# Where GpSimd splits the first half's maxima, and in what order SyncE loads their rows

## The chip, the cores and the metric

The kernel runs on one core of a Trainium2 chip. The core has five engines with an instruction queue each: TensorE (PE in the profile; its weight loads are a row of their own, PEld), VectorE (DVE), ScalarE (ACT), GpSimd (POOL) and SyncE (SP), which in this kernel issues every transfer (DMA). Engines wait for one another through semaphores. The metric is the time of one execution in microseconds (us); lower is better. Times of single instructions are taken from one profiled execution, counted from the start of its span.

## The reference

The program computes a gated mix of attention and a gated linear unit, for one sequence of 2048 tokens of width 512, in 32-bit floats:

```python
x = A_x                                            # 1 x 2048 x 512
g = sigmoid((x * gate_w).sum(-1, keepdims=True))
# a: attention with 32 heads of width 16, a full softmax over 2048 keys
q, k, v = split_heads(x @ wqkv)
p = softmax(einsum("bhqd,bhkd->bhqk", q, k) * 16 ** -0.5)
a = merge_heads(einsum("bhqk,bhkd->bhqd", p, v)) @ wo
# b: gated linear unit, hidden width 1792
b = (sigmoid(x @ w_gate) * (x @ w_up)) @ w_down
return g * a + (1 - g) * b
```

## The kernel before

**Precision.** TensorE works on a reduced 32-bit form. A number is therefore split into a high part h (a cast) and a low part l (the number less h), and a product is made of three matmuls: h by h, h by l, l by h. The splits of weights run on GpSimd, a cast and a subtraction for each buffer (`split_later`, lines 136 and 133).

**Attention.** Heads are taken in 16 pairs. The rows of Q and K of a pair lie in the tiles QS and KS: the first head of the pair in partitions 0 to 63, the second in 64 to 127, so that matmuls of 64 rows for the two heads can run in TensorE's two halves at the same time. For a softmax over 2048 keys the largest score of each query is needed first. `sm_step` computes scores with the queries on the partitions (line 281) and VectorE takes their maxima (line 283) into `stat`. When all 64 maxima of half a pair (8 tiles of 128 queries, 2 heads, 4 blocks of 512 keys) are there, VectorE reduces them once more (line 287) and transposes them (line 289) into a small tile `mt`, which is noted in `mrow`. `put_max` takes it from there: GpSimd splits it into high and low part (line 308 the cast, line 299 the subtraction), SyncE stores the result to memory (`max_d`, line 301) and loads it again, turned into rows, behind the head's rows in QS: four loads (line 305), high and low part for the second head, then for the first. With these rows in place the scores of `st_part` (line 645) come out of TensorE with the maximum already taken off, and ScalarE takes the exponential (line 647).

**The value stage.** Before the main loop comes a stage that computes the values v for all 16 tiles of 128 tokens, two tiles at a time (t = 0, 2, ... 14). It stands at about 35 to 87 us. Each tile is a `Sum` of 12 products, cut into two halves of the contraction, LOW (partitions 0 to 63) and UP. While one tile does its LOW half on one half of TensorE, the other does its UP half on the other; after 12 steps (m = 0 to 11) they change places. Because two halves of TensorE must not write one bank out of turn, `turn` puts an empty GpSimd instruction between, the token (line 170): it waits for the last matmul of the first 12 steps, and the next step's matmuls (line 159) wait for it. Into these steps other work is woven:

- `first_max` issues the first 40 pairs of maxima, at even distances from step 20 of 192 on. The last of the first half of pair 0, (0, 0), falls at t = 12, LOW, m = 9. Right after that step `put_max((0, 0))` is called, which puts its GpSimd instructions in GpSimd's queue ahead of the token of t = 12.
- `work(1.3)` after each 12 steps from t = 12 on takes GpSimd work of an estimated 1.3 us from a list: here the splits of the weights qk1 (two buffers, a cast and a subtraction each).
- `next(ahead)` at t = 14 issues the first four scores of pair 0, for the second head, after the steps LOW 10, UP 1, UP 4 and UP 7. They need the rows of the maxima.

**The main loop** follows, 256 steps of which 246 have the same pattern (`STEADY`): in each, maxima of a later pair, scores and exponentials of the present one, the values' sums (line 778) and six steps for each half of a dense product (`fill`, a list of further products: first more of Q and K, then the hidden layer of the linear unit). The dense products take their weights two buffers at a time (`raw_weights`, line 107 the load, into two buffers that are reused). The loads of the weights qk2 are asked for when the first dense product begins, right ahead of the loop. After the loop comes a tail with the linear unit's second product and the output.

**Queues.** The order of the instructions of TensorE, ScalarE, VectorE and GpSimd is the order of the program. SyncE's is not: a planner orders the transfers by estimated times, within what their dependencies allow. Each queue is in order: an instruction that waits holds all behind it.

Of the kernel before, what the change touches and what calls it, by code (L numbers as in the profile page):

```python
# [22 lines left out]
SYNC = mybir.DependencyInfo(mybir.DependencyClass.Sync, mybir.DependencyReason.DATA)  # L23

S, D, H, DH, F = 2048, 512, 32, 16, 1792
P = 128
KT = D // P
NS = S // P
# [14 lines left out]
LOW, UP = 0, 1  # L43
# [3 lines left out]
def gated_mix(ctx, tc, x, xT, wqk, wv, wo, w_gate, w_up, w_down, gate_w, out):  # L47
    nc = tc.nc
    pe, act, dve, pool, sp = nc.tensor, nc.scalar, nc.vector, nc.gpsimd, nc.sync
# [42 lines left out]
    def big(name, dt=F32):  # L92
        return keep.tile([P, 2048], dt, name=name, tag="big", bufs=4)
# [8 lines left out]
            hi.tensor_copy(h, src)  # L102
        return lo.tensor_tensor(l, src, h.bitcast(F32), ALU.subtract)  # L103

    def raw_weights(src, shape, name):
        raw = keep.tile(shape, F32, name=name + "r", tag="wr", bufs=2)
        sp.dma_start(raw, src)
        return raw, shape, name

    def raw_qk(n, b):  # L110
        return raw_weights(wqk[n, b], [P, 2, 2, P], f"qk{n}_{b}")

    def q_and_k(ws):
        return [[(h[:, i, k, :], l[:, i, k, :]) for h, l in ws for k in range(2)] for i in range(2)]
# [1 line left out]
    def raw_cols(src, n, name):  # L116
        return raw_weights(src[n], [P, KT, P], name)
# [50 lines left out]
    def turn(*runs):  # L168

        token = pool.nop()  # L170
        tc.add_manual_dep(token.ins, runs[-1].last.ins.name, SYNC, reason=SHARED)
        for r in runs:
            r.token = token
# [3 lines left out]
    def work(length):  # L177
        while length > 0.3 and (later or slow):
            cost, step = (later or slow).pop(0)
            step()  # L180
            length -= cost
# [7 lines left out]
    QS, KS = zip(*[(big(f"qs{b}", F32R), big(f"ks{b}", F32R)) for b in range(2)])  # L189
# [57 lines left out]
    raw, xr, w_qk = [], {}, []  # L247
    for b in range(2):
        raw.append(raw_qk(0, b))
        xr[0] = load_x(0, xr.get(0), range(2 * b, 2 * b + 2))  # L250
# [9 lines left out]

    stat = {}
    mrow = {}
    for m in mpads:
        pool.memset(m, 0.0)

# [26 lines left out]
    def put_max(half):  # L292

        p, i = half
        mt = mrow.pop(half)
        hl = keep.tile([P, 2, 32], F32R, name=f"mhl{p}_{i}", tag="mhl", bufs=2)

        def low():
            pool.tensor_tensor(hl[:, 1, :], mt, hl[:, 0, :].bitcast(F32), ALU.subtract)
            d = max_d[2 * p + i]  # L300
            sp.dma_start(d.rearrange("k r a j -> (k r) a j"), hl.bitcast(F32))
            for b in (1, 0):
                for a in range(2):
                    r = 64 * b + 3 * DH + a
                    sp.dma_start(QS[p % 2][r:r + 1, i * 1024:(i + 1) * 1024].rearrange(
                        "o (t k j) -> o t k j", t=8, k=4).bitcast(F32),
                        d[:, 8 * b:8 * b + 8, a, :].rearrange("k t j -> t k j").unsqueeze(0))
        return [(0.2, lambda: pool.tensor_copy(hl[:, 0, :], mt)), (0.25, low)]  # L308
# [63 lines left out]
    def filling():  # L372
# [5 lines left out]
        def raws(kind, n):  # L378
            if kind == "qk":
                return [raw_qk(n, b) for b in range(2)]  # L380
            if kind == "far":
                both = []
                for m in range(2):
                    raw = keep.tile([P, KT, P], F32, name=f"far{m}{n}r", tag="wr", bufs=2)
                    sp.dma_start(raw[:, 2:], gu_w[m][n][:, 2:])
                    both.append(raw)
                return both
            if kind == "down":
                return [raw_weights(w_down[f * P:(f + 1) * P, :], [P, D], f"wd{f}") for f in range(2)]
            if kind == "heads":  # L390
                return [raw_weights(wo[k * P:(k + 1) * P, :], [P, D], f"wo{k}") for k in range(2)]
            m, i = n
            return [raw_cols(gu_w[m], i + a, f"{kind}{m}_{i + a}") for a in (0, HF)]
# [185 lines left out]
    def first_max():  # L579
        if first:  # L580
            j, i = first.pop(0)
            one = sm_step(j)
            one(0, i)
            one(1, i)
# [36 lines left out]
    def tokens(t):  # L621
        return [((xh[:, k, t * P:(t + 1) * P], xl[:, k, t * P:(t + 1) * P]), w_v[k]) for k in range(KT)]

    def put_v(t, o, engine):
        to = v[:, t, :].rearrange("p (h c) -> p h c", c=VW)[:, :, :DH]
        o = o.rearrange("p (h c) -> p h c", c=DH)
        if engine is act:
            act.activation(to, o, AF.Copy)  # L628
        else:
            engine.tensor_copy(to, o)  # L630
# [21 lines left out]
    for t in range(0, NS, 2):  # L652
        two = [Sum(bankv(), tokens(t + a)) for a in range(2)]
        for g in (LOW, UP):
            for m in range(3 * KT):
                if 12 * (t + g) + m >= 20 + (192 - 20) * (2 * LEAD - len(first)) // (2 * LEAD):
                    first_max()
                two[0].half(g)
                two[1].half(1 - g)
                if (0, 0) in mrow:  # L660
                    for _, step in put_max((0, 0)):
                        step()
                if t == NS - 2 and (g, m) in ((LOW, 10), (UP, 1), (UP, 4), (UP, 7)):
                    next(ahead)
            if g == LOW:
                turn(*two)
            if t >= 12:
                work(1.3)
        if t < NS - 2:
            for a in range(2):  # L670
                put_v(t + a, two[a].o, act)
# [165 lines left out]
    for k in range(NPER):  # L837
        n = 2 * k
# [3 lines left out]
        if 78 <= k < 126:  # L842
            t, r = divmod(k - 78, 6)
# [174 lines left out]
```

## Time and profile before

| | |
|---|---|
| time, median of 3 runs | 1697.17 us (1696.29 to 1697.56) |
| the profiled execution's own time | 1697.63 us |
| its span, first to last instruction | 1695.8 us |
| PE busy | 1686.1 us (99%) |
| DVE busy | 1447.3 us (85%) |
| ACT busy | 1357.0 us (80%) |
| POOL busy | 881.5 us (52%) |

The span is 1.8 us shorter than the time of the execution that it belongs to; what lies around it is the start and the end of the program. A row of a timeline gives start, duration, engine, line and operation, the tile written and the tiles read, shapes, a count (x2 is two instructions merged), and in brackets how long the engine had been idle and what ended that. In a table of waits stands who waited for whom, then the total in us, the number of times and the longest. Two rows with the same start are the two halves of TensorE. SPq and POOLq are instructions of those engines' sequencers, such as the issue of a transfer or an empty instruction.

### The profile page before, as it was taken

What the parts mean: (1) busy time and instruction counts of PE and PEld (TensorE: products, weight loads), DVE (VectorE), ACT (ScalarE), POOL (GpSimd) and SP (SyncE); (2) the same over time, 40 slices, a digit from 0 to 9 for tenths busy, and PEclk for the clock granted to TensorE, in tenths of its full rate; (3) what the DMA queues carried; (4) which work ended last, traced back from release to release, by engine and by line L of the source; (5) the groups of instructions that cost most, each with busy time, mean ns of one, the idle gap of its engine ahead of it and who ended that gap; (6) DMA issues with size and microseconds to landing.
All of it is one profiled execution on the core that took longest, in us unless ns stands there. A gap on an engine that the chain in (4) does not pass through costs nothing.

```text
span 1695.8 us, 34520 instructions
## 1 busy us (share of the span) xinstructions
PE 1686.1 (99%) x12509; PEld 1031.9 (61%) x12509; DVE 1447.3 (85%) x2333; ACT 1357.0 (80%) x2643; POOL 881.5 (52%) x862
## 2 busy tenths in 40 slices
PE   9999999999999999999999999999999999999999
PEld 7755555555555556555555555555555555567887
DVE  6888888888889989999888888889988888897643
ACT  4188888888988889888888989889898888974321
POOL 1034343447665555554666667676666767653110
PEclk9999999999999999999999999999999999999999
DMA  7411424253756352543635353535353434378752
GB/s 235 109 40 58 95 64 95 64 126 138 202 170 143 114 119 90 114 114 107 192 100 138 107 144 104 142 108 134 108 126 107 126 120 144 129 239 269 269 195 72
DMA packets 126922, 223.51 MB, mean 132 GB/s; under 512 B 23520, under 2 KB 33504, under 8 KB 123872
## 3 DMA queue, kind: packets, MB, share of 16 engines
q1 hardware_dynamic: 126752, 221.31, 45.1%
q8 instruction: 98, 1.61, 0.4%
q14 instruction: 72, 0.59, 0.1%
HBM read 131.33 MB, written 89.92 MB: 130 GB/s over the span
## 4 chain that ended last, share of the span: by engine, by line
PE 96%; DVE 2%; DMA 1%; issue 0%; ACT 0%; POOL 0%; SPq 0%; POOLq 0%; DVEq 0%; ACTq 0%
PE dn L159 30%; PE sm L778 27%; PE sm L281 12%; PE st L645 7%; PE sm L645 5%; PE sm L963 4%; PE st L281 3%; PE st L159 2%; PE dn L963 2%; PE st L609 1%; PE st L146 1%; PE st L963 1%; DMA gul<-gu_d 1%; PE sm L146 1%; DVE gul L713 0%
## 5 line engine op out<-in xcount | busy, mean ns | idle before, releaser
L283 DVE TENSOR_REDUCE stat<-sm 128x1 f32<-128x512 f32 x1310 | 849.4, 684 | 153.0 <-PE sm L645 127.3
L647 ACT ACTIVATE p<-st 128x512 f32<-128x512 f32 x1020 | 617.8, 652 | 1.9 <-PE st L159 0.9
L647 ACT ACTIVATE p<-sm 128x512 f32<-128x512 f32 x1026 | 608.7, 630 | 0.2 <-PE sm L645 0.2
L281 PE MATMUL sm<-ks,qs 48*128 48x512 f32 x1310 | 515.9, 435 | 0.0
L283 DVE TENSOR_REDUCE stat<-st 128x1 f32<-128x512 f32 x738 | 482.6, 682 | 0.1
L778 PE MATMUL sm<-p,v 128*17 128x512 f32 x4032 | 482.1, 595 | 0.0
L645 PE MATMUL st<-qs,ks 64*128 64x512 f32 x1020 | 427.1, 419 | 0.2 <-DVE stat L283 0.2
L645 PE MATMUL sm<-qs,ks 64*128 64x512 f32 x1026 | 427.0, 419 | 0.1
L281 PEld LDWEIGHTS sm<-ks,qs 48*128 48x128 f32 x1310 | 233.9, 184 | 289.6 <-DVE stat L283 207.7
L795 POOL TENSOR_TENSOR sum<-sum,part 128x512 f32<-128x512 f32 x224 | 288.9, 1290 | 182.1 <-PE sm L645 162.9
L281 PE MATMUL st<-ks,qs 48*128 48x512 f32 x738 | 291.5, 395 | 0.0
L783 ACT ACTIVATE part<-sm 128x512 f32<-128x512 f32 x215 | 128.7, 599 | 132.7 <-issue 106.6
L778 PEld LDWEIGHTS sm<-p,v 128*17 128x17 f32 x4032 | 93.6, 96 | 227.0 <-issue 156.6
L645 PEld LDWEIGHTS st<-qs,ks 64*128 64x128 f32 x1020 | 187.7, 184 | 30.5 <-issue 3.4
L645 PEld LDWEIGHTS sm<-qs,ks 64*128 64x128 f32 x1026 | 189.1, 185 | 9.3 <-issue 4.3
L511 POOL TENSOR_TENSOR chain<-chain,chain 128x512 f32<-128x512 f32 x84 | 108.4, 1290 | 114.7 <-PE sm L645 105.0
L281 PEld LDWEIGHTS st<-ks,qs 48*128 48x128 f32 x738 | 137.7, 187 | 1.3 <-ACT v L628 0.3
L511 POOL TENSOR_TENSOR had<-chain,had 128x512 f32<-128x512 f32 x84 | 108.2, 1288 | 57.2 <-PE sm L645 41.9
L511 POOL TENSOR_TENSOR side<-side,side 128x512 f32<-128x512 f32 x28 | 36.2, 1292 | 92.6 <-PE sm L645 82.6
L573 ACT ACTIVATE chain<-dn 128x512 f32<-128x512 f32 x112 | 77.8, 694 | 0.0
L103 POOL TENSOR_TENSOR ol<-ot,oh 128x1024 fp32r<-128x1024 f32 (+1 forms) x8 | 16.4, 2054 | 100.9 <-ACT oh L100 87.3
L308 POOL CAST mhl<-mt 128x32 fp32r<-128x32 f32 x32 | 7.4, 232 | 104.0 <-DVE mt L289 104.0
(837 smaller groups left out, 3208.4 us busy)
## 6 DMA issues: line engine op xcount, KB each, us to landing
gul<-gu_d SPq DMA_DIRECT2D x56, 512.0 KB
had<-gu_d SPq DMA_DIRECT2D x84, 256.0 KB
gu_d<-had SPq DMA_DIRECT2D x84, 256.0 KB
gu_d<-side SPq DMA_DIRECT2D x56, 256.0 KB
qs<-q_d SPq DMA_DIRECT2D x90, 128.0 KB
ks<-k_d SPq DMA_DIRECT2D x90, 128.0 KB
pv_d<-sum SPq DMA_DIRECT2D x32, 256.0 KB
gu_d<-far SPq DMA_DIRECT2D x28, 256.0 KB
```

The costliest lines, as they stand in the source:

```text
L146: pe.matmul(o, a, b, start=(i == 0), stop=(i == len(ops) - 1))
L159: mm = pe.matmul(self.o, a[rows], b[rows], start=(self.n == 0), stop=(self.n == 2 * len(self.ops) - 1))
L281: pe.matmul(t, qs[r:r + KM, qt * P:(qt + 1) * P], ks[r:r + KM, g * 512:(g + 1) * 512], start=True, stop=True)
L283: dve.tensor_reduce(stat[half][:, b, qt % 8, g:g + 1], t, axis=AX.X, op=ALU.max)
L511: pool.tensor_tensor(to, u, w, ALU.add)
L573: leave = lambda e, o: act.activation(e, o, AF.Copy)
L645: pe.matmul(o, ks[r:r + KR, (kt + a) * P:(kt + a + 1) * P], qs[r:r + KR, q0:q0 + 512], start=True, stop=True)
L647: act.activation(pt[:, 2 * a + c, :], o, AF.Exp, scale=DH ** -0.5)
L778: pe.matmul(o[32 * c:32 * c + VW, :], v[:, 2 * k % 16 + a, h * VW:(h + 1) * VW], pts[c // 2][:, 2 * a + c % 2, :], start=(a == 0), stop=(a ...
L783: act.activation(e, o, AF.Copy)
L795: pool.tensor_tensor(s, s, e, ALU.add)
L963: pe.matmul(down[t], a, b, start=(f == 0 and m == 0), stop=(f == NF - 2 and m == 5))
```

## The change

It has four parts:

1. `put_max((0, 0))` is called at t = 12 after the step UP, m = 2, in place of right after LOW, m = 9. GpSimd's split of the first half's maxima so stands behind the token of t = 12 in its queue.
2. GpSimd's work from the list is taken in two portions of 2.6 at the step UP, m = 6 of t = 12 and t = 14, in place of four portions of 1.3 after each 12 steps.
3. The two loads of the weights qk2 get a dependency on the last of the four loads of the maxima's rows of (0, 0), so that they wait until it has landed.
4. The first four scores are issued after the steps LOW 11, UP 2, UP 5 and UP 8, each one step later.

```diff
-    def raw_weights(src, shape, name):
+    def raw_weights(src, shape, name, behind=None):
         raw = keep.tile(shape, F32, name=name + "r", tag="wr", bufs=2)
-        sp.dma_start(raw, src)
+        load = sp.dma_start(raw, src)
+        if behind is not None:
+            tc.add_manual_dep(load.ins, behind.ins.name, SYNC, reason="weights behind the rows of the maxima")
         return raw, shape, name

     def raw_qk(n, b):
-        return raw_weights(wqk[n, b], [P, 2, 2, P], f"qk{n}_{b}")
+        return raw_weights(wqk[n, b], [P, 2, 2, P], f"qk{n}_{b}", rows_in[0, 0] if n == 2 else None)
...
+    rows_in = {}
...
-                    sp.dma_start(QS[p % 2][r:r + 1, i * 1024:(i + 1) * 1024].rearrange(
+                    rows_in[p, i] = sp.dma_start(QS[p % 2][r:r + 1, i * 1024:(i + 1) * 1024].rearrange(
...
                 two[0].half(g)
                 two[1].half(1 - g)
-                if (0, 0) in mrow:
+                if (0, 0) in mrow and g == UP and m == 2:
                     for _, step in put_max((0, 0)):
                         step()
-                if t == NS - 2 and (g, m) in ((LOW, 10), (UP, 1), (UP, 4), (UP, 7)):
+                if t == NS - 2 and (g, m) in ((LOW, 11), (UP, 2), (UP, 5), (UP, 8)):
                     next(ahead)
+                if t >= 12 and m == 6 and g == UP:
+                    work(2.6)
             if g == LOW:
                 turn(*two)
-            if t >= 12:
-                work(1.3)
```

## The prediction

> **What bounds the kernel now.** I read the page first for its busy shares, then the table of waits for TensorE (PE) alone, then PE's busy time by stretches, then the timelines of the few microseconds in which the waits stand, and last the chain of waits there. The page:
>
> ```profile
> span 1695.8 us, 34520 instructions
> PE 1686.1 (99%) x12509; PEld 1031.9 (61%) x12509; DVE 1447.3 (85%) x2333; ACT 1357.0 (80%) x2643; POOL 881.5 (52%) x862
> ```
>
> PE is busy for 1686.1 of 1695.8 us. This change removes no matmul, so all it can take away is idle time of PE, of which there are 1695.8 - 1686.1 = 9.7 us in the whole program. The table of waits says what ended the idle times (who waited, for whom: us in total, times, longest):
>
> ```profile
> PE dn L159 <- POOLq L170: 1.6, 1, 1.6
> ...
> PE dn L645 <- DMA qs<-max_d: 0.9, 1, 0.9
> ```
>
> These are the two places that the change touches: a half sum of the value stage (L159) that waits for GpSimd's token (L170), and the first score (L645) that waits for the loads of the maxima's rows (DMA qs<-max_d). Together that is 2.5 us, 0.15% of the time. The windows' busy times show where nothing is left to take (stretch, its length, busy time of PE with its count, then the other engines):
>
> ```profile
> 87.27:1460.00 1372.73, 1372.51 (x10802) 795.01 (x10802) 1224.00 (x2066) 1220.16 (x2439) 808.68 (x810) 1.00 0.43 119
> ```
>
> From the first step of the main loop on, PE is busy 1372.51 of 1372.73 us. Whatever is gained or lost ahead of 87.27 us goes straight through this stretch to the end, because PE's own order sets it.
>
> Now PE's timeline at both places (start, duration, engine, line, operation):
>
> ```profile
> 65.46 0.40 PE L159 MATMUL st<-wv_h,xl 64*128 64x512 f32 x2
> 65.97 0.50 PE L159 MATMUL st<-wv_h,xh 64*128 64x512 f32 x2
> ...
> 72.34 0.39 PE L159 MATMUL st<-wv_l,xh 64*128 64x512 f32 x1
> 72.57 0.39 PE L159 MATMUL st<-wv_h,xl 64*128 64x512 f32 x1
> 74.58 0.50 PE L159 MATMUL dn<-wv_h,xh 64*128 64x512 f32 x1 [1.61 <-POOLq L170]
> 74.92 0.39 PE L281 MATMUL sm<-ks,qs 48*128 48x512 f32 x2
> ...
> 80.94 0.39 PE L159 MATMUL st<-wv_l,xh 64*128 64x512 f32 x2
> 82.22 0.47 PE L645 MATMUL dn<-qs,ks 64*128 64x512 f32 x1 [0.89 <-DMA qs<-max_d]
> 82.56 0.58 PE L159 MATMUL st<-wv_h,xl 64*128 64x512 f32 x2
> 83.25 0.51 PE L159 MATMUL st<-wv_h,xh 64*128 64x512 f32 x2
> ```
>
> Step m of a half is one such row; a row starts 0.23 us after the last (72.34 to 72.57). Between LOW's last step and UP's first stands the token. It cost 65.97 - 65.46 = 0.51 us at t=10, but 74.58 - 72.57 = 2.01 us at t=12. Why, the other engines say (DVE, POOL and SP in the order of time):
>
> ```profile
> 73.98 0.21 DVE L289 STREAM_TRANSPOSE mt<-mpad 128x32 f32<-128x32 f32 x1
> 74.26 0.21 POOL L308 CAST mhl<-mt 128x32 fp32r<-128x32 f32 x1 [55.39 <-DVE mt L289]
> 74.55 0.25 POOL L299 TENSOR_TENSOR mhl<-mt,mhl 128x32 fp32r<-128x32 f32 x1
> 74.83 0.34 SPq L301 DMA_DIRECT2D max_d<-mhl  x1
> 75.44 1.29 POOL L133 TENSOR_TENSOR qk_0l<-qk_0r,qk_0h 128x512 fp32r<-128x512 f32 x1
> 76.75 0.35 SPq L107 DMA_DIRECT2D qk_0r<-in_wqk_dram  x1
> 77.36 1.29 POOL L133 TENSOR_TENSOR qk_1l<-qk_1r,qk_1h 128x512 fp32r<-128x512 f32 x1
> 78.67 0.33 SPq L107 DMA_DIRECT2D qk_1r<-in_wqk_dram  x1
> 79.10 2.90 SPq L305 DMA_DIRECT2D qs<-max_d  x4
> ```
>
> GpSimd's cast L308 waits for VectorE's transposed maxima (mt, ready at 73.98 + 0.21 = 74.19), and the token behind it in POOL's order waits too. SyncE issues the store of the maxima at 74.83, then two weight loads, each only once GpSimd has read the buffer that it overwrites (76.73 and 78.65), and only then the four row loads. The chain of waits at this place (start, duration, what), which goes on with the score at 82.22:
>
> ```profile
> 77.36 1.30 POOL qk_1l L133
> 78.67 0.33 SPq L107
> 79.10 0.80 SPq L305
> 79.95 2.13 DMA qs<-max_d
> ```
>
> **The change, part by part.**
>
> The token (split moved behind UP's step m=2 at t=12). The token then waits only for LOW's last matmul, as at t=10: 0.51 instead of 2.01 us, a gain of 1.50. The cast itself stays at 74.26, since the transposed maxima set it and they depend on matmuls ahead of the token. VectorE's next maxima come 1.50 us sooner (matmul at 73.42 instead of 74.92), while it is at the final reduction until 74.19; it has a backlog then, and it does not shrink, because a maximum takes 0.62 us (next fence: ten in 6.23 us), two take 1.24, and two are asked for every 172 / 40 = 4.3 steps and their own, 5.3 x 0.23 = 1.22 us. But VectorE starts them at 74.3 at the earliest, 0.9 us after the matmul, and the four banks allow PE one such pair more, 1.22 us, ahead of it. So I count nothing; if PE had to wait for a bank, it would be tenths of a microsecond.
>
> ```profile
> 75.35 6.23 DVE L283 TENSOR_REDUCE stat<-sm 128x1 f32<-128x512 f32 x10 [1.16 <-PE sm L281]
> ...
> 122.27 0.33 SPq L301 DMA_DIRECT2D max_d<-mhl  x1
> ...
> 124.80 0.68 SPq L305 DMA_DIRECT2D qs<-max_d  x1
> ```
>
> The row loads. The store is issued at 74.83 as before. At the second such pair (fence above) the first row load follows 124.80 - 122.27 = 2.53 us after the store, which I take for the store's landing; so here it goes out at 74.83 + 2.53 = 77.36 instead of 79.10. The second row load follows 79.95 - 79.10 = 0.85 later, 78.21, and from it to the released score are 82.22 - 79.95 = 2.27 us. The rows of the first scores are there at 80.48 instead of 82.22.
>
> The first scores one step later. PE reaches LOW's m=10 at 80.94 - 1.50 = 79.44. Then come two maxima, m=11 and the score, 0.23 each: the score is ready at 79.44 + 0.69 = 80.13 and waits until 80.48, 0.35 us. After such a wait the next pair of matmuls came 82.56 - 82.22 = 0.34 later, so UP's first step starts at 80.82. The token costs nothing there: m=11 starts at 79.90, and 79.90 + 0.51 = 80.41 is earlier. Before, UP's first step started at 83.25. The three parts together gain 83.25 - 80.82 = 2.43 us. With rows that land at once the token would set it, 83.25 - 80.41 = 2.84. With rows that land no sooner than now, 82.22 + 0.34 = 82.56, the gain is 0.69.
>
> The Trainium skill, "DMA: Bandwidth & Descriptors", section "Latency and other measured facts", says that the fixed cost of a DMA is mostly the round trip to memory and becomes smaller with a lighter memory load. By that rule the row loads, with no weights in flight beside them, should land in less than the 2.27 us of the trace, and the sum would move from 2.43 towards 2.84; no run so far shows it, and I keep 2.43.
>
> What is behind the new wait. The first weight load waits for the last row load, and SyncE's queue behind it. That queue has nothing more to issue until 100.59; the other rows of this fence are the first readers of what comes later now, and ScalarE at the end of the value stage:
>
> ```profile
> 86.55 0.60 ACT L647 ACTIVATE p<-st 128x512 f32<-128x512 f32 x1 [0.56 <-PE st L645]
> 87.46 1.08 ACT L628 ACTIVATE v<-st 128x512 f32<-128x512 f32 x2 [0.32 <-PE st L159]
> 93.66 0.40 PE L159 MATMUL dn<-xh,qk_1h 64*128 64x512 f32 x1
> ...
> 100.59 0.38 SPq L233 DMA_DIRECT2D q_d<-qe  x1
> ...
> 124.12 0.60 POOL L136 CAST qk_0h<-qk_0r 128x512 fp32r<-128x512 f32 x1
> ```
>
> The last row load goes out two places behind the second, at 78.21 + 2 x 0.73 = 79.7 (four took 2.90 us), and lands by 82; GpSimd reads the weights at 124.12, so 40 us cover them. The work of 2.6 at m=6 takes the two splits (0.60 + 1.29 each) in three operations and one: the first three go behind the row split of t=12, from 74.80 to 77.3, ahead of t=14's token (79.90 + 0.39 = 80.3); the fourth, qk_1l, goes behind that token and ends near 81.6. TensorE first uses qk_1 at 93.66, 91.2 with the gain taken off. So both cost nothing, with 9 us of cover; without it, 1.29 us for the late operation. The last score comes 0.23 us later against the end of its stage, and its exponential on ScalarE, which ended at 86.55 + 0.60 = 87.15, then ends 0.08 us short of the copy of the last value tiles at 87.46. That costs nothing; an exponential that is 0.1 us later still would cost about as much.
>
> Sum: 1697.63 us was the profiled execution (span 1695.8), 0.46 over the median of 1697.17. A gain of 2.43 gives 1695.2 against the profiled execution's own time and 1694.7 against the median. The bounds above give 1694.3 (rows at once) and 1696.5 (rows no sooner).
>
> **Rivals.**
>
> The rows come no sooner. Then the score's wait swallows most of what the token gains. It would be so if the store's landing took 82.22 - 80.48 = 1.74 us longer than at 122.27, or if the planner of SyncE's queue kept something ahead of the rows. For it: the landing of the store at 74.83 itself is not shown. Against it: the manual dependency leaves no other transfer in the queue there. Gain 0.69, time 1696.5.
>
> Slower: SyncE's queue is not in program order. The loads of a head pair are planned by estimates, and a shifted estimate could move one behind a longer wait at one of the 14 later pair changes. Pair 2's loads and the longest wait of that queue:
>
> ```profile
> 181.88 4.64 SPq L242 DMA_DIRECT2D ks<-k_d  x6
> ...
> SPq L233 <- POOL qe L133: 152.4, 23, 18.5
> ```
>
> They are issued by 186.5; pair 2's maxima start 22 steps of 1372.73 / 246 = 5.58 us after 87.27, near 210, so some 21 us of lead are left after a landing like the 2.53 above. One wait of 18.5 is covered; it decides only where a load falls behind two, and one such stall of about 2 x 18.5 - 21 = 16 us would give 1697.2 - 2.4 + 16 = 1711. From 5.8 us on the kernel is slower by 0.2%.
>
> Faster than the sum: the main loop gets tighter, because ScalarE's backlog in its first step or VectorE's phase is another. Against it: PE idles for only 0.22 us of that stretch, so it would have to come from matmuls that overlap better. But 0.004 us on each of 246 steps is 1 us, and with that the time is 1693.7.
>
> **How the numbers follow.** What a measurement of this kernel can tell from no change is about 0.2%, 3.4 us, and the whole PE idle time that the change addresses is less. The sum as worked out, 0.63, with 1694.2 to 1695.6 as its own range; rows no sooner, 0.16; the planner's loss, 0.09; the tighter loop, 0.12, most of it below 1693.8. So faster by over 0.2% 0.12, within 0.78, slower 0.10. The range is 1693.6 to 1697.0: it takes in the bounds and half of the tighter loop.
>
> **What would show it.** The wait of PE for POOLq L170 goes from the table, and VectorE's idle of 1.16 us ahead of 75.35 with it. SyncE's order reads store, four row loads, two weight loads, with the first row load near 77.4. The score's wait for qs<-max_d is at most 0.35 us, and the main loop's first matmul stands near 84.8 instead of 87.27. The prediction is wrong if that point moves by 2.4 us and the end doesn't, if the rows leave SyncE later than 78, or if PE waits for DVE stat in the value stage.

## The result and the profile after

The changed kernel takes 1694.22 us (median of 22 runs, 1693.27 to 1698.36) against 1697.06 us for the kernel before (22 runs, 1696.29 to 1699.51): a ratio of 0.9985, with a 95% interval of 0.9978 to 0.9991. That is 2.84 us by the medians, faster by 0.15% by the ratio and within the 0.2% that the prediction calls no change. The forecast was 1694.7.

The table of PE's waits after (who waited, for whom: us in total, times, longest), whole:

```profile
PE st L84 <- DVE warm L80: 0.9, 1, 0.9
PE sm L648 <- DMA qs<-max_d: 0.3, 1, 0.3
PE sm L284 <- DVE stat L286: 0.3, 1, 0.3
PE dn L966 <- POOL wd5l L103: 0.3, 1, 0.3
PE st L648 <- DVE stat L286: 0.2, 1, 0.2
```

Lines of the file have moved by two or three: L161 is the value stage, L172 the token, L648 the scores, L308 the row loads. The wait of 1.6 for the token is gone. A wait for qs<-max_d is still there, but it is another one: it stands at 1466.79 us, at the end of the loop, and writes sm, not dn. The first score waits for nothing. The two waits for VectorE's maxima (DVE stat) stand at 842.60 and 1451.33 us, none in the value stage. PE's timeline at the two places:

```profile
72.78 0.39 PE L161 MATMUL st<-wv_h,xl 64*128 64x512 f32 x1
73.29 0.50 PE L161 MATMUL dn<-wv_h,xh 64*128 64x512 f32 x1
...
79.67 0.39 PE L161 MATMUL st<-wv_l,xh 64*128 64x512 f32 x2
79.89 0.40 PE L284 MATMUL sm<-ks,qs 48*128 48x512 f32 x2
80.13 0.40 PE L161 MATMUL st<-wv_h,xl 64*128 64x512 f32 x2
80.36 0.39 PE L648 MATMUL dn<-qs,ks 64*128 64x512 f32 x1
80.64 0.50 PE L161 MATMUL st<-wv_h,xh 64*128 64x512 f32 x2
...
84.66 0.47 PE L284 MATMUL sm<-ks,qs 48*128 48x512 f32 x1
```

Between LOW's last step and UP's first at t=12 are now 73.29 - 72.78 = 0.51 us. At t=14 the pair of maxima, the last step and the score follow one another at 0.23 us, and UP's first step comes 0.51 us after LOW's last, with the score in between. The other engines:

```profile
74.19 0.21 DVE L292 STREAM_TRANSPOSE mt<-mpad 128x32 f32<-128x32 f32 x1
74.32 7.29 DVE L286 TENSOR_REDUCE stat<-sm 128x1 f32<-128x512 f32 x12
74.46 0.21 POOL L311 CAST mhl<-mt 128x32 fp32r<-128x32 f32 x1 [55.24 <-DVE mt L292]
75.04 0.34 SPq L304 DMA_DIRECT2D max_d<-mhl  x1
76.51 2.91 SPq L308 DMA_DIRECT2D qs<-max_d  x4
80.75 0.36 SPq L107 DMA_DIRECT2D qk_0r<-in_wqk_dram  x1
80.78 1.29 POOL L135 TENSOR_TENSOR qk_1l<-qk_1r,qk_1h 128x512 fp32r<-128x512 f32 x1 [3.28 <-PE dn L648]
82.09 0.34 SPq L107 DMA_DIRECT2D qk_1r<-in_wqk_dram  x1
```

SyncE's order is store, four row loads, two weight loads, and the first row load leaves 76.51 - 75.04 = 1.47 us after the store. VectorE's idle of 1.16 us is gone: its reductions follow the transposition without a break.

The whole stage begins up to 0.7 us earlier or later from one execution to another (here LOW's last step at t=12 is at 72.78 against 72.57), so I compare stretches inside one trace: from that step to the main loop's first matmul. It was 87.27 - 72.57 = 14.70 us and is 84.66 - 72.78 = 11.88: 2.82 us less. A second execution of the kernel before, the last of the experiments, has 14.52, so this figure is good to about 0.2 us, and that the medians give 2.84 too is luck in the second decimal.

The two profiled spans differ by more, 1695.8 against 1692.5. The main loop starts 2.61 us sooner in the profile after and keeps that to 2.4 until 1385 us; its last steps give back 0.9, so that 1.48 are left at the last sums of values (1502.47 against 1500.99; two of the waits above stand there, 0.3 each). The tail takes 187.3 us from the start of those sums to the start of the last matmul, against 189.2. The profile of before had a wait there that no edit touches and that the profile after lacks:

```profile
PE sm L963 <- DVE hl L103: 1.3, 2, 1.0
```

SyncE, GpSimd, VectorE and ScalarE run the same sequence of operations in both kernels from the first to the last, tokens aside, but for the place of the two weight loads.

### The profile page after: what moved, and what is told of

The parts are those of the page before. It is cut to its first block, busy times and chain, and to the rows that moved or that the text cites. A ratio compares the mean times of both kernels' runs of the same rounds, so it can differ in the third digit from the quotient of the medians.

```text
span 1692.5 us, 34518 instructions
## 1 busy us (share of the span) xinstructions
PE 1685.8 (100%) x12509; PEld 1032.5 (61%) x12509; DVE 1446.7 (85%) x2333; ACT 1357.4 (80%) x2643; POOL 880.7 (52%) x862
## 4 chain that ended last, share of the span: by engine, by line
PE 96%; DMA 1%; DVE 1%; POOL 1%; issue 0%; SPq 0%; ACT 0%; POOLq 0%; DVEq 0%
PE dn L161 30%; PE sm L781 27%; PE sm L284 12%; PE st L648 7%; PE sm L966 5%; PE sm L648 5%; PE st L284 2%; PE dn L966 2%; PE st L161 2%; PE st L966 2%; PE st L148 1%; PE st L612 1%; PE sm L148 1%; DVE stat L286 1%; DMA gul<-gu_d 1%
## 5 line engine op out<-in xcount | busy, mean ns | idle before, releaser
L648 PE MATMUL sm<-qs,ks 64*128 64x512 f32 x1026 | 426.9, 419 | 0.3 <-DMA qs<-max_d 0.3
L648 PE MATMUL st<-qs,ks 64*128 64x512 f32 x1020 | 426.9, 419 | 0.2 <-DVE stat L286 0.2
L648 PEld LDWEIGHTS st<-qs,ks 64*128 64x128 f32 x1020 | 187.7, 184 | 30.2 <-issue 3.4
L648 PEld LDWEIGHTS sm<-qs,ks 64*128 64x128 f32 x1026 | 189.1, 185 | 9.5 <-issue 4.3
```

Of the source, the lines that this page charges most:

```text
L648: pe.matmul(o, ks[r:r + KR, (kt + a) * P:(kt + a + 1) * P], qs[r:r + KR, q0:q0 + 512], start=True, stop=True)
```

## The experiments

The table has the stretch of each kernel, from LOW's last step at t=12 to the main loop's first matmul (14.70 before), and the median time, with the ratio to the kernel before and its 95% interval. The times can't tell these kernels from one another; the stretches can, where they differ by more than the 0.18 us between the two executions of the kernel before.

| kernel | stretch, us | gain in it | median, us | ratio (interval) |
|---|---|---|---|---|
| changed kernel | 11.88 | 2.82 | 1694.22 | 0.9985 (0.9978 to 0.9991) |
| dependency alone | 13.60 | 1.10 | 1696.12 | 0.9996 (0.9986 to 1.0005) |
| later scores alone | 13.75 | 0.95 | 1696.11 | 0.9992 (0.9982 to 1.0001) |
| split and work moved alone | 12.83 | 1.87 | 1694.98 | 0.9987 (0.9978 to 0.9996) |
| changed, old scores | 12.25 | 2.45 | 1694.86 | 0.9989 (0.9979 to 0.9998) |
| changed, no dependency | 11.92 | 2.78 | 1693.96 | 0.9981 (0.9972 to 0.9990) |
| changed, old places of work | 11.86 | 2.84 | 1693.76 | 0.9985 (0.9975 to 0.9994) |
| changed, a load beside the store | 12.99 | 1.71 | 1695.02 | 0.9987 (0.9977 to 0.9996) |
| kernel before, once more | 14.52 | 0.18 | 1697.2 (one run) | |

**The dependency alone.** Edit, on the kernel before: the new argument of `raw_weights` and `rows_in`, as in the change's diff, and

```diff
-        return raw_weights(wqk[n, b], [P, 2, 2, P], f"qk{n}_{b}")
+        return raw_weights(wqk[n, b], [P, 2, 2, P], f"qk{n}_{b}", rows_in[0, 0] if n == 2 else None)
```

> Only the dependency of the two weight loads on the row loads is added; split, work and scores stay as before. The stretch from LOW's last step at t=12 to the main loop's first matmul is 14.70 us before and 11.88 in the changed kernel. Theory (three parts that each have a place on the path): the token still costs 2.01, the row loads leave about 1.5 us after the store at 74.83 and land by 79.5, so the first score at 81.17 waits for nothing; UP's first step moves from 83.25 to about 82.1 and the stretch is 13.6. Rival (the rows come no sooner): the wait for qs<-max_d stays 0.9 and the stretch 14.7.

Measured: the stretch is 13.60. The table of its waits still has 1.6 us for the token, and in its PE timeline the first score follows LOW's m=10 without a wait:

```profile
81.60 0.39 PE L161 MATMUL st<-wv_l,xh 64*128 64x512 f32 x2
81.82 0.39 PE L648 MATMUL dn<-qs,ks 64*128 64x512 f32 x1
```

The rival, rows that come no sooner, falls. This execution had the tail's wait for VectorE too (1.0 us).

**The later scores alone.** Edit, on the kernel before:

```diff
-                if t == NS - 2 and (g, m) in ((LOW, 10), (UP, 1), (UP, 4), (UP, 7)):
+                if t == NS - 2 and (g, m) in ((LOW, 11), (UP, 2), (UP, 5), (UP, 8)):
```

> Only the first four scores are one step later; split, work and loads stay as before. Theory: the token of t=12 still costs 2.01 and the rows land at 82.2; the score waits one step less, and the step's matmul and the token of t=14 hide behind its wait, so UP's first step starts at about 82.6 instead of 83.25 and the stretch is 14.0. Rival (the step's place is worth nothing by itself): 14.7.

Measured: 13.75, a quarter of a microsecond better than expected. The rows of its waits, ahead of 90 us, whole:

```profile
PE dn L159 <- POOLq L170: 1.6, 1, 1.6
PE dn L645 <- DMA qs<-max_d: 0.3, 1, 0.3
```

The step does two things. The wait for the rows falls from 0.9 to 0.3, because a pair of maxima and a step of the half sums stand ahead of it now, and the token of t=14 passes meanwhile.

**Split and work moved, nothing else.** Edit, on the kernel before:

```diff
-                if (0, 0) in mrow:
+                if (0, 0) in mrow and g == UP and m == 2:
...
+                if t >= 12 and m == 6 and g == UP:
+                    work(2.6)
             if g == LOW:
                 turn(*two)
-            if t >= 12:
-                work(1.3)
```

> Only the split of the maxima and the weights' splits on GpSimd are moved; no dependency, first scores at the old steps. Theory: the token costs 0.51. SyncE's planner puts the first weight load ahead of the rows and the second behind them, since its buffer is now read late; the row loads leave at about 77.1 and land by 80.3, the score, ready at 79.67, waits 0.3 to 0.6, and the stretch is 12.6 to 12.8. Rival (without the dependency the rows gain nothing, and the wait swallows the token's gain): rows land at 82.2, the stretch is 14.5 or more.

Measured: 12.83, just above the theory's 12.6 to 12.8; the rival's 14.5 falls. SyncE's and PE's timelines:

```profile
75.55 0.34 SPq L301 DMA_DIRECT2D max_d<-mhl  x1
77.48 0.35 SPq L107 DMA_DIRECT2D qk_0r<-in_wqk_dram  x1
77.92 2.91 SPq L305 DMA_DIRECT2D qs<-max_d  x4
83.55 0.34 SPq L107 DMA_DIRECT2D qk_1r<-in_wqk_dram  x1
...
81.05 0.47 PE L645 MATMUL dn<-qs,ks 64*128 64x512 f32 x1 [0.48 <-DMA qs<-max_d]
```

One weight load stays ahead of the rows. The other goes behind them without any dependency, since its buffer is read by the last of GpSimd's operations, which now stands behind the token of t=14. The three parts' gains one by one are 1.87 + 1.10 + 0.95 = 3.92 us, and together 2.82: the dependency and the later scores shorten the same wait.

**The changed kernel with the scores at their old steps.** Edit: the later-scores diff above, undone.

> The changed kernel with the first four scores at their old steps. Theory: the rows are there in time even for the earlier step, and all that is lost is that the first score no longer runs while the token of t=14 is under way: 0.23 us, a stretch of 12.1 instead of 11.88 and no wait for qs<-max_d above 0.1. Rival (the later step is needed for the rows to land, as the prediction's sum had it): a wait for qs<-max_d of 0.3 to 0.8 and a stretch of 12.3 to 12.8.

Measured: 12.25, a loss of 0.37, between the theory's 12.1 and the rival's 12.3. No wait over 0.15 us is noted for the rows; the score starts 0.33 us after LOW's m=10 instead of 0.23, so it was held for at most 0.1. UP's first step starts 1.37 us after LOW's m=10, against 0.97 in the changed kernel. The rival's wait of 0.3 to 0.8 isn't there; that the score fills the token's time is the larger part of what the later step brings.

**The changed kernel without the dependency.** Edit: the dependency's diff, undone.

> The changed kernel without the dependency of the weight loads on the row loads. Theory (the dependency moves only one of the two weight loads, since the second already waits for a buffer that is read late): SyncE issues the first weight load ahead of the rows, which leave about 0.9 us later than in the changed kernel; the score waits 0.1 to 0.2 us and the stretch is 12.0 to 12.15 instead of 11.88. Rival (the dependency is what brings the rows forward): both weight loads ahead, the rows 2 us later or more, a stretch of 13.5 or more.

Measured: 11.92, 0.04 more than the changed kernel, less than expected. Its PE timeline says why:

```profile
80.27 0.40 PE L159 MATMUL st<-wv_h,xl 64*128 64x512 f32 x2
80.64 0.46 PE L645 MATMUL dn<-qs,ks 64*128 64x512 f32 x1
80.79 0.55 PE L159 MATMUL st<-wv_h,xh 64*128 64x512 f32 x2
```

The score is held until 80.64, 0.14 us after its turn, and yet UP's first step starts 0.52 us after LOW's last: a wait of the score that is shorter than the token's time costs next to nothing, because the token takes that time anyway. So the dependency is worth 1.10 us by itself, and behind the other parts 0.04, which is not more than two executions differ by.

**The changed kernel with GpSimd's work at its old places.** Edit: the two hunks with `work` above, undone.

> The changed kernel with the weights' splits in four portions after each 12 steps, as before. Theory: the first two operations (0.61 and 1.29 us) now stand between the token of t=12 and the cast of the maxima on GpSimd, so the cast starts about 0.85 us later (near 75.3 instead of 74.46) and with it the store and the rows; the rows land at 80.4 to 80.7 with the score ready at 80.36, and the stretch is 11.9 to 12.3. Rival (GpSimd's other work has no part in it): cast at 74.46 and a stretch of 11.88.

Measured: 11.86, no loss. GpSimd's timeline shows the split of the weights ahead of the cast of the maxima, which starts at 75.72, 1.26 us later than in the changed kernel (0.35 of that is this execution's later stage):

```profile
74.49 1.29 POOL L135 TENSOR_TENSOR qk_0l<-qk_0r,qk_0h 128x512 fp32r<-128x512 f32 x1
75.72 0.22 POOL L311 CAST mhl<-mt 128x32 fp32r<-128x32 f32 x1
```

The cast is 0.9 us late as the theory said, and the rows are still there in time, though only just: the score starts 0.26 us after LOW's last step, where 0.23 is the step, and 2.93 us after the first row load (77.77 to 80.70). How much the changed kernel has to spare depends on the execution: it has 3.85 us from the first row load to the score (76.51 to 80.36), of which this run needed 2.93 and the run with the old scores, whose score was held for 0.1, needed 3.45 (76.95 to 80.40). That is 0.4 to 0.9 us, which the prediction's sum did not have.

**A load beside the store.** On the changed kernel, a second load of gate_w, with the same values, right ahead of the store of the maxima:

```diff
-            pool.tensor_tensor(hl[:, 1, :], mt, hl[:, 0, :].bitcast(F32), ALU.subtract)
+            low = pool.tensor_tensor(hl[:, 1, :], mt, hl[:, 0, :].bitcast(F32), ALU.subtract)
             d = max_d[2 * p + i]
+            if (p, i) == (0, 0):
+                more = sp.dma_start(gwb, gate_w.unsqueeze(0).to_broadcast([P, D]))
+                tc.add_manual_dep(more.ins, low.ins.name, SYNC, reason="a load beside the store of the maxima")
             sp.dma_start(d.rearrange("k r a j -> (k r) a j"), hl.bitcast(F32))
```

> The changed kernel with one more load of 256 KB (gate_w once more, the same values) issued right ahead of the store of the maxima. It tells apart why the store landed in 1.46 us here and in 2.52 at the pair that the prediction took. Theory (the landing grows with other transfers in flight): the first row load leaves 2.0 to 2.5 us after the store, the rows land at 80.7 to 81.0, the score waits 0.3 to 0.6 us and the stretch is 12.2 to 12.5. Rival (2.52 was no landing but SyncE's own delay): the first row load leaves 1.5 us after the store, and the stretch is 11.9.

Measured: 12.99. SyncE's and PE's timelines:

```profile
74.95 0.35 SPq L305 DMA_DIRECT2D gwb<-in_gate_w_dram  x1
75.34 0.43 SPq L307 DMA_DIRECT2D max_d<-mhl  x1
78.44 2.89 SPq L311 DMA_DIRECT2D qs<-max_d  x4
...
80.00 0.40 PE L161 MATMUL st<-wv_h,xl 64*128 64x512 f32 x2
81.44 0.46 PE L651 MATMUL dn<-qs,ks 64*128 64x512 f32 x1 [1.03 <-DMA qs<-max_d]
81.44 0.69 PE L161 MATMUL st<-wv_h,xh 64*128 64x512 f32 x2
```

The first row load leaves 78.44 - 75.34 = 3.10 us after the store instead of 1.47, and the score waits 1.03 us. The theory holds in kind, with a larger effect than expected, and at this place the rival falls. (At the prediction's own pair both are at work; see the part on the row loads below.) Where the time goes, the DMA packets say. The first line counts those that start in the 1.56 us behind the store's issue in the changed kernel (75.04 to 76.60), the second in this one (75.34 to 76.90):

```profile
DMA packets 144, 0.03 MB, mean 21 GB/s; under 512 B 144, under 2 KB 144, under 8 KB 144
DMA packets 72, 0.15 MB, mean 95 GB/s; under 512 B 0, under 2 KB 0, under 8 KB 72
```

The store's packets are those under 512 bytes. In the changed kernel all 144 of them start in that time, in this run not one: only packets of the load do. No packet starts in the last 0.3 us ahead of the first row load in either. So the whole delay lies ahead of the store's last packet, and none of it behind. That fits a store that waits behind the load's packets; which of the 16 DMA engines carries a packet the trace does not say, so the order within one is not shown.

**The last value copy on VectorE**, an attempt at a faster version. Edit, on the changed kernel:

```diff
-    put_v(NS - 2 + a, two[a].o, act)
+    put_v(NS - 2 + a, two[a].o, (act, dve)[a])
```

> The changed kernel with the copy of the last value tile on VectorE instead of ScalarE, an attempt at a faster version. The main loop's first step takes 4.24 us to its first sum of values (4.2 in both kernels) because two banks come free one after the other, 0.49 us apart. Theory: with both copies at the same time the second bank is free 0.5 us sooner and the step gets 0.2 to 0.4 us shorter. Rival (VectorE's maxima are late by the copy's 0.6 us instead): no gain, 4.2 to 4.5.

Measured: from the main loop's first matmul at 85.02 to the first sum of values at 89.12 are 4.10 us against 4.21 to 4.25 in the other eleven profiles, and 1694.63 us in the median. The gain is 0.14 us against the changed kernel's 4.24, between the theory and the rival, and too small for the times.

**Maxima at the token**, a second attempt. Edit, on the changed kernel:

```diff
-                if 12 * (t + g) + m >= 20 + (192 - 20) * (2 * LEAD - len(first)) // (2 * LEAD):
+                if 12 * (t + g) + m >= due(2 * LEAD - len(first)):
...
+    MOVED = {37: 36, 58: 60, 63: 64, 106: 104, 110: 108, 131: 132, 157: 156}
+
+    def due(n):
+        at = 20 + (192 - 20) * n // (2 * LEAD)
+        return MOVED.get(at, at)
```

Five of the seven entries move a pair to UP's first step (36, 60, 108, 132, 156); the other two move a neighbour by one or two steps.

> An attempt at a faster version from what the first scores showed: a matmul that needs no token, put between LOW's last step and UP's first, runs while the token is under way. In the changed kernel one pair of maxima stands there by chance (t=6, 0.50 us from step to step with the pair in between, against 0.51 without). Here five more pairs (t=2, 4, 8, 10, 12) are shifted by one or two steps to stand there. Theory: each such place gains the pair's own 0.23 us, some 1.1 us in all, most of it ahead of t=12's boundary; the time falls about 1.1 us below the changed kernel's 1694.2, to 1693.1, and the main loop's first matmul stands near 83.6 against 84.66. Rival (VectorE is as busy as PE there and takes the gain back through the four banks): 0 to 0.3 us.

Measured: 1692.69 us in the median (10 runs), a ratio to the kernel before of 0.9977, with an interval of 0.9968 to 0.9986. It is the fastest of all, 4.1 us below the kernel before by medians taken together, though its interval overlaps that of the changed kernel. One of the shifted places (t=4) in its PE timeline:

```profile
58.38 0.39 PE L161 MATMUL dn<-wv_h,xl 64*128 64x512 f32 x1
58.60 0.39 PE L284 MATMUL sm<-ks,qs 48*128 48x512 f32 x2
58.88 0.49 PE L161 MATMUL dn<-wv_h,xh 64*128 64x512 f32 x1
```

From LOW's last step to UP's first are 0.50 us with a pair of maxima in between, against 0.51 without one. The windows' busy times of both kernels up to the main loop (the changed kernel, then this one) tell the same:

```profile
35.00:84.66 49.66, 49.08 (x408) 37.85 (x405) 47.38 (x79) 8.79 (x16) 4.16 (x6) 1.00 0.42 109
```

```profile
35.00:84.00 49.00, 49.00 (x412) 38.25 (x409) 47.73 (x80) 9.11 (x17) 4.14 (x6) 1.00 0.47 113
```

PE idled for 0.58 us in that stretch and does not any more; that is about half of the gain. The main loop starts at 84.00 instead of 84.66, and the stage itself began 0.53 us later in this execution (its matmul that started at 33.98 in the changed kernel started at 34.51), so against the stage's start the loop comes 0.66 + 0.53 = 1.2 us sooner, as the theory had it. The rival falls: no wait of PE for VectorE's maxima stands in the value stage.

**The kernel before once more.**

> The kernel before once more, unchanged, for the part that no edit touches: from the last sums of values to the last matmul it takes 197.7 us in the profile of before and 195.8 in that of the changed kernel, because TensorE waits 1.3 us for VectorE there in the one and not in the other. Theory (that difference lies between executions): a time near 195.8 in this execution is as likely as 197.7, and the stretch from LOW's last step to the main loop is 14.7 again. Rival (the tail's wait belongs to the kernel before): 197.7 again.

Measured: 1697.2 us; from the start of the last sums of values to that of the last matmul 188.3 us, between 189.2 and 187.3. (The expectation's 197.7 and 195.8 count from sums 8.5 us earlier; the difference is the same.) The stretch is 14.52, not 14.70 again. The table of its waits has no wait for VectorE's hl, but a longer one for GpSimd's weights:

```profile
PE dn L159 <- POOLq L170: 1.6, 1, 1.6
...
PE dn L963 <- POOL wd5l L103: 0.9, 1, 0.9
PE dn L645 <- DMA qs<-max_d: 0.7, 1, 0.7
```

So one kernel's tail takes two values in two executions, and the rival falls. Over all twelve profiles it takes 187.2 to 189.2 us, and only the two longest, the kernel before and the dependency alone, have the wait for VectorE's hl. That is too few to say how often it comes. The two waits that the change addresses are there again.

## Why the prediction was right

**The token** was right: 0.51 us in place of 2.01, with the cast of the maxima where it was. So was the cover on VectorE: its twelve reductions follow each other for 7.29 us, and no wait of PE for a bank stands there.

**The row loads** were right in order and wrong in time. The step that failed is the term "124.80 - 122.27 = 2.53 us after the store, which I take for the store's landing". Here it was 1.47. The row was the wrong one to take, for two reasons that the trace of before shows at that pair. SyncE's queue had a store of Q (q_d) between the store of the maxima and the row loads; it was issued at 124.19, for 0.36 us, so that no row load could leave before 124.55, however soon the store landed. Four of the next five pairs with such a store between have 2.37 to 2.40 us. And the landing itself was slow, since the row load still waited 0.2 us for it (the first line, from SyncE's waits between 122 and 125 us). The second line, from the DMA queues between 122.27 and 124.00, shows what else was in flight, a transfer of a queue that the profile calls instruction:

```profile
SPq L305 <- DMA max_d<-mhl: 0.2, 1, 0.2
q8 instruction: 1, 0.02, 4.1%
```

Such transfers go with slow landings throughout. In the trace of before SyncE issues nothing between the store and the first row load at 21 of 32 half pairs. At fifteen of them the row load leaves 1.44 to 1.48 us after the store, at six 1.74 to 2.51. At these six, and at none of the fifteen, an instruction transfer starts between 0.2 us ahead of the store's issue and 1.0 us behind it. In all twelve profiles there are 76 stores with such a transfer, at 1.74 to 3.05 us, and 183 without, 171 of them at 1.56 or less. The others lie between 1.63 and 1.98, but for the 3.10 beside the added load. At the changed place no instruction transfer was in flight. That it is the transfer which slows the store is argued from this agreement; no run moves one.

The Trainium skill's rule that the prediction set beside its row ("DMA: Bandwidth & Descriptors", "Latency and other measured facts": a lighter memory load, a smaller fixed cost) has the direction of the store's landing, 1.47 us alone and 3.10 beside a load. Its reason, the round trip to memory, is not what these runs show: the delay lay ahead of the store's packets, not behind them. For the row loads, to which the prediction applied it, no run shows it: from the issue of the second row load to the held score are 2.27 us before, 2.26 in the run with the split moved alone, with one weight load just ahead of the rows, and 2.15 and 2.59 in two runs with none (the added load and the old scores).

**The later scores** were right in kind. The score waits for nothing, and the token is the limit, so the gain is 2.82, next to the 2.84 that the prediction gave as the bound for rows that land at once, and not 2.43. A second error of the sum was hidden behind the first: it let UP's first step wait 0.34 us behind a late score. The row that it took, at 82.56, is not the next pair of matmuls after the score. The trace of before has a pair of maxima there, which starts together with the score:

```profile
82.22 0.70 PE L281 MATMUL sm<-ks,qs 48*128 48x512 f32 x2
```

In the two runs in which UP's first step stands right behind a score that waits longer than the token, it starts together with the score too (82.63 with the later scores alone, 81.44 with the added load), and the main loop's first matmul comes 4.23 and 4.24 us after the score. The sum had 0.34 and then 87.27 - 83.25 = 4.02, together 4.36. So this error took 0.13 off the forecast gain, and the store's landing the rest of the way from 2.43 to 2.84. Without the dependency the score was 0.14 us late and UP's first step came 0.15 us after it, in step with the token.

**What costs nothing** cost nothing. The weights' splits at their old places make no difference (11.86 against 11.88). The later operation and the weight loads delayed nobody: no such wait is in the table.

**The rivals.** Rows that come no sooner did not happen in any run with the split moved or the dependency. The planner's loss did not happen: SyncE's 1054 transfers have the same order in both profiles but for the two weight loads. The main loop got no tighter: of the 2.61 us at its start 2.4 are left at 1385 us.

The time, 1694.22, lies 0.5 us below the forecast of 1694.7. The mis-sized terms account for 2.82 - 2.43 = 0.39 of it. That the time agrees so closely is in part luck: the medians of single kernels here differ by as much without a change in the stretch (1693.76 and 1694.22 at 11.86 and 11.88).

## What to carry to other kernels

When a landing time is needed, take it from many rows of the same transfer, leave out those at which the queue was held by something else, and look at what was in flight, instruction transfers too. The prediction's one row, 2.53 us, had both against it; fifteen of the 21 clean ones have 1.44 to 1.48. When a row is taken for what comes next after a wait, look at every row between. Parts of a change that shorten the same wait are not to be added: singly these three gained 3.9 us, together 2.8, and the dependency, worth 1.1 us alone, was worth almost nothing behind the others. Where two halves of TensorE hand over through another engine, a matmul that needs no hand-over, put into the gap, was free here (0.50 us against 0.51); doing so at five more places gained 1.2 us, about as much as the dependency alone.

## What was not expected of the hardware

A store of 32 KB that lands in 1.47 us with nothing else in flight took 3.10 us with one load of 256 KB issued 0.39 us ahead of it, and its packets had not begun 1.56 us after its issue. A transfer of the profile's instruction queues goes with a slow landing as well: of the same stores, 76 with one close by took 1.74 to 3.05 us, while 171 of 183 without took at most 1.56. No line of the kernel issues such a transfer, and the row that the prediction took had one beside it.

And a matmul of one of TensorE's halves that waits holds back the other half. In the run with the added load, UP's first step starts at 81.44 together with the late score, although one of its two matmuls uses the half that the score leaves free. The last step ahead of the token stands at 80.00, and the token's time is 0.51 us elsewhere. The program puts that step behind the score, and TensorE took it in that order.
